# A kernel of block attention and a feed-forward network whose planner is given other durations and preferences

## The chip, the core and the metric

The kernel runs on one core of a Trainium2 chip. The core has five engines that run side by side, each through its own list of instructions in order: TensorE (PE) multiplies matrices and transposes, ScalarE (ACT) applies functions and copies, VectorE (DVE) does elementwise work, reductions and 32 x 32 transposes, GpSimd (POOL) does elementwise work and issues some transfers, and SyncE (SP) issues most transfers (DMA). Engines wait for each other by semaphores. The metric is the time of one execution on the device in microseconds (us), lower being better.

## The reference

The inputs q, k and v are 8 x 8 x 576 x 64 float32 numbers (batch, heads, sequence, head size), the weights 512 x 2048 and 2048 x 512. The weights come as float64 arrays, which the kernel receives as 8-byte words and turns into float32 itself.

```python
scores = scale * np.matmul(q_c, k_c.transpose(0, 1, 2, 4, 3))   # blocks of 64 positions
scores = scores - np.max(scores, axis=-1, keepdims=True)
attn = np.exp(scores)
attn = attn / (np.sum(attn, axis=-1, keepdims=True) + 1e-09)
out = np.matmul(attn, v_c)
...
x = np.ascontiguousarray(attn_out.transpose(0, 2, 1, 3)).reshape(B * S, H * D)
...
h = x @ w_in
g = h * (1.0 / (1.0 + np.exp(-1.702 * h)))
return (g @ w_out).astype(np.float32)
```

Each block of 64 positions attends to itself alone. The 4608 rows of the result, 512 wide, go through a feed-forward network of width 2048.

## The kernel before

**Tiles.** The 4608 rows are 36 tiles of 128 rows, in nine blocks of four tiles. The width 2048 is 16 slices j of 128. For a block n and a slice j, numbered g = 16 n + j, the kernel makes h (128 x 512), its activation g, and adds four products, one per tile of the block, to four output accumulators. A float32 product is made of three: each operand is split into a high part and a low rest (`g_h` and `g_l`, `x_h` and `x_l`, two halves of `w`), and high x high, high x low and low x high are summed. Blocks 0 to 2 are computed plainly. The other six go in twos, where seven products (`P1` to `P7`, line 698 on) take the place of eight.

**Names of steps.** Each step has a name by which the text speaks of it. For the first four attention tiles u: `q_u`, `k_u`, `v_u` are loads (256 KB each, line 368), `tqp_u` and `tkp_u` transposes on PE (line 407), `tq_u` and `tk_u` the copies of these (lines 412, 416 on ACT, 418 on DVE), `s_u` the scores (line 428), `m_u`, `sm_u` maximum and subtraction on DVE, `ex_u` the exponential on ACT (441), `z_u` the sum (445 to 448), `n_u` the division on POOL (451), `ep_u` the transposes of the weights of attention on PE (456), `et_u` their copy (463), `xp_u` the product with v (472), and `xh_u`, `xl_u` its two parts (480, 483). From tile 4 on, tiles go in pairs with like names; their rows come by `rows0_4` and `rows1_4` and are transposed by `tp0_4` and `tp1_4` (891) in pair 4, and in later pairs they come in small loads `qk_i_n_u` (866) that DVE transposes (`tq0_u`, `tq1_u`, 909). From pair 8 on `s_u` also holds the product with v of the pair before. For the weights of slice j: `raw_j` is two loads (288 and 292, 512 KB each), `wsc_j` and `wlow_j` two steps on ACT (296, 300), `wshift_j` and `wj_j` two on DVE (305, 309), `wh_j` one on ACT (314) and `w_j` the last on DVE (319). For the feed-forward: `h0_g` and `h_g` are halves of the first product (1160 to 1162; for the first two slices 1171 to 1173, by halves of the columns, `h_0_0` the very first), `gh_g` the activation and its high part (1181, 1182), `gl_g` the rest (1187), and `o_g_t` the product for tile t (1197 to 1199). `fill_0` to `fill_2` and `warm` are matmuls without use, which keep PE busy (1272); `gt` loads the table of the activation (1276).

**What sets the order.** All steps are handed to a planner, class `Plan`, with engine, an assumed duration, a rank, the steps that they need and the buffers that they take and give. `emit` (line 99) plays the plan through: whenever an engine is free it takes, of the steps whose needs are met and whose buffers are free, the one with the lowest rank. A step's end is told to other engines `HANDOVER` later. The resulting sequence is the program order of every engine; the hardware takes no part in it and an engine that meets a step whose input isn't there waits, with everything behind it. Two tables bend the order: `NUDGE` adds to the rank of single steps, `SHIFT` to those of a whole pair. For the first 20 to 50 steps of each engine the table `ORDER` (line 22) writes the order out.

```python
rank += self.nudge.get(make, 0.0) + self.shift
...
turn = name == first[e][-1] if first.get(e) else name not in listed
if turn and all(self.free[b] >= take.count(b) for b in take):
    pick = i
...
plan.add(DMA, (2, 1.5, 384), rank - 5.5, load, need=need, make=e("raw"), take=[f"w{j}"])
plan.add(ACT, 1.08, rank, scale, need=[e("raw")], make=e("wsc"))
```

## Time and profile before

| what | value |
|---|---|
| median of 3 runs | 825.58 us (823.32 to 827.49) |
| profiled execution | 828.46 us, its span 826.7 us |
| instructions in the span | 14873 |
| granted TensorE clock | 1.000 |
| DMA moved | 114.24 MB, mean 138 GB/s |

The span goes from the first to the last instruction; 1.8 us of the profiled execution lie around it. A row of the timeline has start, length, engine, line of the program, operation, what is written from what, shape and number of instructions, and in brackets idle time of the engine before it and what ended it. PE's lengths are modelled, and neighbours overlap, so the text counts from start to start.

### The profile page before, as it was taken

The page shows a single profiled execution, that of the slowest core. Times are in us where ns is not written, and L with a number is a line of the kernel's source. Part 1 is how long each engine was busy: PE and PEld are TensorE (multiplying, and loading weights), DVE is VectorE, ACT ScalarE, POOL GpSimd, SP SyncE. Part 2 cuts the span into 40 slices and gives each one's busy share as a digit, 9 for nine tenths or more (in the row PEclk, how much of TensorE's full clock was granted, in tenths as well). Part 3 has the DMA queues.
Part 4 walks back from the last instruction along what each step waited for, and adds up shares of the span by engine and source line. Part 5 has one row for each costly group of instructions (what it writes and reads, how often), then busy time and mean ns, then how long its engine had stood idle before and what let it go on. Part 6 is the DMA issues. An engine that isn't in the chain of part 4 may idle for free.

```text
span 826.7 us, 14873 instructions
## 1 busy us (share of the span) xinstructions
PE 814.1 (98%) x5750; PEld 673.2 (81%) x5750; DVE 525.8 (64%) x725; ACT 370.9 (45%) x545; POOL 137.7 (17%) x170
## 2 busy tenths in 40 slices
PE   8899999999999999999999999999999999999998
PEld 7778787888888888888888888888888888888886
DVE  5868975664487768873958874857568443443422
ACT  5989745323445537433436434434454323222322
POOL 1000172112176422030203030200010010000100
PEclk9999999999999999999999999999999999999999
DMA  8997855532385356756655255655440054444101
GB/s 214 334 278 218 291 156 126 90 60 39 71 270 155 82 169 198 180 144 171 165 155 144 51 102 166 155 142 144 122 141 26 1 178 127 117 117 123 52 1 51
DMA packets 219237, 114.24 MB, mean 138 GB/s; under 512 B 172640, under 2 KB 195424, under 8 KB 219168
## 3 DMA queue, kind: packets, MB, share of 16 engines
q1 hardware_dynamic: 214624, 103.20, 47.4%
q0 software_dynamic: 4544, 10.10, 3.7%
q8 instruction: 45, 0.74, 0.4%
q14 instruction: 24, 0.20, 0.1%
HBM read 89.13 MB, written 24.12 MB: 137 GB/s over the span
## 4 chain that ended last, share of the span: by engine, by line
PE 82%; SPq 9%; DMA 4%; ACT 2%; DVE 2%; issue 1%; POOL 0%; DVEq 0%
PE po L1197 14%; PE po L1199 14%; PE po L1198 14%; PE hp L710 9%; PE hp L712 9%; PE hp L711 9%; PE hp L1160 3%; PE hp L1161 3%; PE hp L1162 3%; DMA raw<-in_moe_w_out_dram 3%; SPq L368 2%; SPq L288 2%; SPq L866 2%; PE s L925 2%; PE x L999 2%; SPq L292 1%
## 5 line engine op out<-in xcount | busy, mean ns | idle before, releaser
L1197 PE MATMUL po<-w,g_l 128*128 128x512 f32 x576 | 226.4, 393 | 0.3 <-DVE g_l L1187 0.2
L1199 PE MATMUL po<-w,g_h 128*128 128x512 f32 x576 | 224.3, 389 | 0.0
L1198 PE MATMUL po<-w,g_h 128*128 128x512 f32 x576 | 224.3, 389 | 0.0
L1197 PEld LDWEIGHTS po<-w,g_l 128*128 128x128 f32 x576 | 108.1, 188 | 23.8 <-DVE g_l L757 0.5
L1199 PEld LDWEIGHTS po<-w,g_h 128*128 128x128 f32 x576 | 108.1, 188 | 22.7
L1198 PEld LDWEIGHTS po<-w,g_h 128*128 128x128 f32 x576 | 108.1, 188 | 21.8
L710 PE MATMUL hp<-w,w 128*128 128x512 f32 x224 | 87.2, 389 | 0.0
L712 PE MATMUL hp<-w,w 128*128 128x512 f32 x224 | 87.1, 389 | 0.0
L711 PE MATMUL hp<-w,w 128*128 128x512 f32 x224 | 87.1, 389 | 0.0
L974 DVE STREAM_TRANSPOSE eT<-e 32x512 f32<-32x512 f32 x120 | 84.2, 702 | 4.6 <-POOL e L955 2.7
L748 ACT ACTIVATE g<-g 128x512 f32<-128x512 f32 x48 | 30.1, 632 | 124.8 <-DVE g L695 124.4
L1160 PE MATMUL hp<-x_l,w 128*128 128x512 f32 x184 | 72.1, 392 | 1.6 <-DVE g_l L1187 1.5
L1161 PE MATMUL hp<-x_h,w 128*128 128x512 f32 x184 | 71.6, 389 | 0.0
L1162 PE MATMUL hp<-x_h,w 128*128 128x512 f32 x184 | 71.6, 389 | 0.0
L1216 POOL DMA_DIRECT2D out_dram<-ob x35 | 19.4, 557 | 294.7 <-DVE ob L1211 222.8
L753 ACT ACTIVATE g_h<-g 128x512 fp32r<-128x512 f32 x48 | 30.3, 630 | 72.5 <-PE po L1199 71.4
L757 DVE TENSOR_TENSOR g_l<-g,g_h 128x512 fp32r<-128x512 f32 x48 | 33.1, 690 | 44.4 <-ACT g_h L753 44.1
L1187 DVE TENSOR_TENSOR g_l<-hp,g_h 128x512 fp32r<-128x512 f32 (+1 forms) x50 | 33.2, 665 | 37.9 <-ACT g_h L1182 37.6
L909 DVE STREAM_TRANSPOSE qkT<-raw 128x1024 f32<-128x1024 f32 x30 | 36.9, 1237 | 27.7 <-PE s L925 18.1
L866 POOL DMA_DIRECT2D raw<-in_k_dram x44 | 26.3, 600 | 151.7 <-DMA v<-in_v_dram 80.3
L710 PEld LDWEIGHTS hp<-w,w 128*128 128x128 f32 x224 | 42.0, 188 | 8.9 <-ACT d L723 0.2
L712 PEld LDWEIGHTS hp<-w,w 128*128 128x128 f32 x224 | 42.0, 188 | 8.7
(120 smaller groups left out, 1254.3 us busy)
## 6 DMA issues: line engine op xcount, KB each, us to landing
w<-seven SPq DMA_DIRECT2D x112, 256.0 KB, 2.8
pieces<-seven SPq DMA_DIRECT2D x56, 256.0 KB, 2.8
seven<-w SPq DMA_DIRECT2D x24, 512.0 KB, 4.0
raw<-in_moe_w_in_dram SPq DMA_DIRECT2D x16, 512.0 KB, 7.4
raw<-in_moe_w_out_dram SPq DMA_DIRECT2D x16, 512.0 KB, 7.7
out_dram<-ob POOLq DMA_DIRECT2D x27, 256.0 KB, 2.6
raw<-in_q_dram SPq DMA_DIRECT2D x208, 32.0 KB, 2.2
v<-in_v_dram SPq DMA_DIRECT2D x26, 256.0 KB, 3.4
```

The source lines that it names most:

```text
L710: nc.tensor.matmul(hp, w[:, 0, c], xl[:, c], start=c == 0, stop=False)
L711: nc.tensor.matmul(hp, w[:, 0, c], xh[:, c], start=False, stop=False)
L712: nc.tensor.matmul(hp, w[:, 1, c], xh[:, c], start=False, stop=c == 1)
L866: queue.dma_start(t[p0 : p0 + 32, i, n, o // 32 : (o + c) // 32, :], src[b, 2 * n + h, s : s + c, d * 32 : d * 32 + 32].rearrange("(t j) i ...
L909: nc.vector.transpose(st["tr"][:, i].rearrange("p n (t j) -> p (n t) j", j=32), st["raw"][:, i].rearrange("p n t j -> p (n t) j"),)
L974: nc.vector.transpose(st["et"][po : po + 32, :, 32 * a : 32 * a + 32], st["e"][pi : pi + 32, :, 32 * b : 32 * b + 32],)
L1160: nc.tensor.matmul(hp, wh, xl, start=cc == 0, stop=False)
L1161: nc.tensor.matmul(hp, wh, xh, start=False, stop=False)
L1162: nc.tensor.matmul(hp, wl, xh, start=False, stop=cc == NCC - 1)
L1197: nc.tensor.matmul(po, gl[:, c], w[:, 0, :], start=first, stop=False)
L1198: nc.tensor.matmul(po, gh[:, c], w[:, 0, :], start=False, stop=False)
L1199: nc.tensor.matmul(po, gh[:, c], w[:, 1, :], start=False, stop=last)
```

## The change

The durations that the planner assumes are changed for some twenty kinds of steps (by -0.3 to +0.6 us); and a step on ACT or DVE now holds its engine 0.08 less, while its result counts for other engines 0.20 after that (0.12 before) and for its own engine 0.08 after it. `NUDGE` gets some twenty new entries, `SHIFT` has twelve instead of six, and `ORDER` is written anew. No instruction is added, removed or altered.

```diff
@@ ORDER, ACT @@
-        "tk_1 tq_1 tq_0 ex_1 tq_2 tk_2 ex_0 tq_3 tk_3 ex_2 et_1 wsc_0 wlow_0 xh_1 ex_3 et_0 et_2 "
+        "tq_1 tk_1 tq_0 tk_2 ex_1 tq_2 tq_3 ex_0 wsc_0 wlow_0 tk_3 ex_2 et_1 xh_1 ex_3 wsc_1 et_0 "
...
@@ ORDER, DMA @@
-        "k_1 q_1 k_0 q_0 q_2 k_2 q_3 k_3 raw_0 v_1 v_0 v_2 raw_1 v_3 raw_3 raw_2 rows0_4 raw_4 "
+        "q_1 q_0 k_1 k_0 k_2 q_3 q_2 raw_0 k_3 v_1 raw_1 v_3 v_2 v_0 rows0_4 raw_3 raw_2 raw_4 "
...
-    HANDOVER = {None: 0.0, PE: 0.25, ACT: 0.12, DVE: 0.12, POOL: 0.15, DMA: 0.1}
+    HANDOVER = {None: 0.0, PE: 0.25, ACT: 0.2, DVE: 0.2, POOL: 0.15, DMA: 0.1}
+    OVERLAP = {ACT: 0.08, DVE: 0.08}
...
+        if engine in self.OVERLAP:
+            cost -= self.OVERLAP[engine]
...
-                        post(done + late, 1, (make, e, True))
+                        post(done + late + self.OVERLAP.get(e, 0.0), 1, (make, e, True))
...
+        "o_123_3": 8.5, "P3_2_7": 8, "wsc_12": -1, "qk_1_2_10": 2, "d3_0_0": 1, "h0_18": 1, "t4x_2_0": -2,
     }
-    SHIFT = {10: 3.5, 8: 2.0, 26: -12.5, 12: 4.0, 34: -12.5, 6: 3.0}
+    SHIFT = {10: 1.5, 8: 2.0, 26: -12.5, 12: 4.0, 34: -3.0, 6: 2.0, 32: 9.0, 18: -9.0, 30: 12.5, 22: 2.0, 28: 16.5, 20: 1.0}
...
-        plan.add(DMA, (2, 1.5, 384), rank - 5.5, load, need=need, make=e("raw"), take=[f"w{j}"])
+        plan.add(DMA, (2, 1.6, 384), rank - 5.5, load, need=need, make=e("raw"), take=[f"w{j}"])
```

Three places show what the new order does. Six lines were put in near the top of the program, so a line L296 of before is L302 in the changed kernel, and so on. In the rows the first number in a tile's name is the tile or slice.

SP's list of transfers at the beginning, from the eighth one on; before:

```order
L368 DMA first_a_3_121<-in_k_dram 128x8x64
L288 DMA raw_0_157<-in_moe_w_in_dram 128x4x128
L292 DMA raw_0_157<-in_moe_w_out_dram 128x512
L368 DMA first_b_1_150<-in_v_dram 128x8x64
L368 DMA first_b_0_188<-in_v_dram 128x8x64
L368 DMA first_b_2_225<-in_v_dram 128x8x64
L288 DMA raw_1_274<-in_moe_w_in_dram 128x4x128
L292 DMA raw_1_274<-in_moe_w_out_dram 128x512
L368 DMA first_b_3_298<-in_v_dram 128x8x64
```

and now:

```order
L294 DMA raw_0_129<-in_moe_w_in_dram 128x4x128
L298 DMA raw_0_129<-in_moe_w_out_dram 128x512
L374 DMA first_a_3_113<-in_k_dram 128x8x64
L374 DMA first_b_1_170<-in_v_dram 128x8x64
L294 DMA raw_1_178<-in_moe_w_in_dram 128x4x128
L298 DMA raw_1_178<-in_moe_w_out_dram 128x512
L374 DMA first_b_3_223<-in_v_dram 128x8x64
L374 DMA first_b_2_236<-in_v_dram 128x8x64
L374 DMA first_b_0_189<-in_v_dram 128x8x64
```

The first weights go ahead of k_3, the second ahead of three of the v loads, and v_0 from second to last of these.

ACT's list at the same place, from ex_0 on (line 441 before, 447 now; tile 0); before:

```order
L441 ACTIVATE first_b_0_188<-first_b_0_188 128x512
L412 ACTIVATE first_a_3_121<-qkTp_3_0_190 128x512
L416 ACTIVATE first_a_3_121<-qkTp_3_1_220 128x512
L441 ACTIVATE first_b_2_225<-first_b_2_225 128x512
L463 ACTIVATE first_b_1_150<-eTp_1_232 128x512
L296 ACTIVATE raw_0_157<-raw_0_157 128x1024
L300 ACTIVATE raw_0_157<-raw_0_157 128x1024
L480 ACTIVATE x_h_0_83<-x_1_281 128x4x128
L441 ACTIVATE first_b_3_298<-first_b_3_298 128x512
L463 ACTIVATE first_b_0_188<-eTp_0_301 128x512
```

and now:

```order
L447 ACTIVATE first_b_0_189<-first_b_0_189 128x512
L302 ACTIVATE raw_0_129<-raw_0_129 128x1024
L306 ACTIVATE raw_0_129<-raw_0_129 128x1024
L422 ACTIVATE first_a_3_113<-qkTp_3_1_231 128x512
L447 ACTIVATE first_b_2_236<-first_b_2_236 128x512
L469 ACTIVATE first_b_1_170<-eTp_1_251 128x512
L486 ACTIVATE x_h_0_83<-x_1_288 128x4x128
L447 ACTIVATE first_b_3_223<-first_b_3_223 128x512
L302 ACTIVATE raw_1_178<-raw_1_178 128x1024
L469 ACTIVATE first_b_0_189<-eTp_0_280 128x512
```

wsc_0 and wlow_0, the two steps on raw_0, stand ahead of tk_3, ex_2 and et_1 now, and wsc_1 ahead of et_0.

PE's list around tp1_4, the transposes of pair 4's second rows; before:

```order
L1197 MATMUL po_0_3_533<-w_3_543,g_l_3_630 128x512
L1198 MATMUL po_0_3_533<-w_3_543,g_h_3_629 128x512
L1199 MATMUL po_0_3_533<-w_3_543,g_h_3_629 128x512
L891 MATMUL qkTp_4_1_671<-ident_73,rows_4_330 128x128 x8
L1160 MATMUL hp_5_686<-x_l_0_84,w_5_644 128x512
```

and now:

```order
L897 MATMUL qkTp_4_1_661<-ident_73,rows_4_306 128x128 x8
L1203 MATMUL po_0_3_498<-w_3_563,g_l_3_617 128x512
L1204 MATMUL po_0_3_498<-w_3_563,g_h_3_616 128x512
L1205 MATMUL po_0_3_498<-w_3_563,g_h_3_616 128x512
L1166 MATMUL hp_4_620<-x_l_0_84,w_4_583 128x512
```

o_3_3 and the second half of h of slice 4 (h_4, six matmuls, of which the last row is the first) come behind the transposes now; before, both came ahead of them.

More of the change, by code (lines that the diff above doesn't have):

```diff
@@ L487, in plan_first @@
         rank = u - 95
[L488 to L492 removed]
+        plan.add(DMA, (1, 1.05, 1024), u - 103, lambda: load(0), make=ev("q"), take=[slot(0)])
+        plan.add(DMA, (1, 1.05, 1024), u - 102.9, lambda: load(1), make=ev("k"))
+        plan.add(DMA, (1, 1.05, 1024), u - 101.5, load_v, make=ev("v"), take=[slot(1)])
+        plan.add(PE, 0.62, rank, lambda: t_pe(0), need=[ev("q")], make=ev("tqp"), take=["hp"])
+        plan.add(PE, 0.62, rank, lambda: t_pe(1), need=[ev("k")], make=ev("tkp"), take=["hp"])
         plan.add(ACT, 0.55, rank, t_q, need=[ev("tqp")], make=ev("tq"), give=["hp"])
         plan.add(ACT if k_act else DVE, 0.62, rank, t_k, need=[ev("tkp")], make=ev("tk"), give=["hp"])
[L495 removed]
+        plan.add(PE, 1.08, rank + 0.6, s_pe, need=[ev("tq"), ev("tk")], make=ev("s"), take=[f"po{u}"], give=[slot(0)])
         plan.add(DVE, 0.71, rank + 0.6, s_max, need=[ev("s")], make=ev("m"))
@@ L639, in plan_prep @@
             plan.bulk((1.5, 0.85)[i], first - PREP, lambda i=i: out_a(i), need=[(w0, w1)[i]], make=outs[i])
-        plan.add(POOL, 1.05, rank, lambda: whole(0), need=[w0, f"w_{NF - 1}"], make=e("pa0"), take=["tmp"])
-        plan.add(POOL, 1.05, rank, lambda: whole(1), need=[w1, e("pa0")], make=e("pa"))
-        plan.add(POOL, 2.4, rank, sums, need=[e("pa")], make=e("psum"), take=["tmp"], give=["tmp"])
+        plan.add(POOL, 1.27, rank, lambda: whole(0), need=[w0, f"w_{NF - 1}"], make=e("pa0"), take=["tmp"])
+        plan.add(POOL, 1.27, rank, lambda: whole(1), need=[w1, e("pa0")], make=e("pa"))
+        plan.add(POOL, 3.0, rank, sums, need=[e("pa")], make=e("psum"), take=["tmp"], give=["tmp"])
         for i in range(2):
@@ L761, in plan_two @@
             at = rank + STEP * i / 7
-            plan.bulk(0.72, at - LEAD, lambda k=k, i=i: load(k, i), need=[f"po_{p}"], make=e(f"ld{i}"), take=[f"piece{k}"])
+            plan.bulk(0.8, at - LEAD, lambda k=k, i=i: load(k, i), need=[f"po_{p}"], make=e(f"ld{i}"), take=[f"piece{k}"])
             xneed = [f"l{OPERANDS[name][1]}x_{s}_{h}" for h in range(2)] if p == 0 else []
@@ L765, in plan_two @@
             plan.add(
-                PE, 1.36, at - 0.2, lambda k=k, i=i: product(k, i), need=[e(f"ld{i}"), before] + xneed, make=e(name),
+                PE, 1.362, at - 0.2, lambda k=k, i=i: product(k, i), need=[e(f"ld{i}"), before] + xneed, make=e(name),
                 take=["hp"], give=[f"piece{k}"],
@@ L1092, in plan_pair @@
             plan.add(
-                PE, 2.2, rank + 0.6, lambda: (s_pe(), last["x"][0]()), need=both + [ev("hp0"), ev("hp1")],
+                PE, 2.04, rank + 0.6, lambda: (s_pe(), last["x"][0]()), need=both + [ev("hp0"), ev("hp1")],
                 make=ev("s"), take=["att", "att", "e"], give=["tr", "et", "v"],
@@ L1101, in plan_pair @@
         plan.add(DVE, 1.65, rank + 0.6, s_sum, need=[ev("ex")], make=ev("z"))
-        plan.add(POOL, 2.0, rank + 0.6, s_norm, need=[ev("z")], make=ev("n"))
+        plan.add(POOL, 1.9, rank + 0.6, s_norm, need=[ev("z")], make=ev("n"))
         if pe:
-            plan.add(PE, 0.95, rank + 1.7, e_pe, need=[ev("n")], make=ev("ep"), take=["att", "att"], give=["e"])
+            plan.add(PE, 0.82, rank + 1.7, e_pe, need=[ev("n")], make=ev("ep"), take=["att", "att"], give=["e"])
             plan.add(ACT, 1.05, rank + 1.7, e_act, need=[ev("ep")], make=ev("et"), take=["et"], give=["att", "att"])
@@ L1114, in plan_pair @@
             plan.add(
-                PE, 1.4, rank + 1.5, x_pe, need=part["x"][1], make=ev("xp"), take=bank, give=["et", "v"],
+                PE, 1.1, rank + 1.5, x_pe, need=part["x"][1], make=ev("xp"), take=bank, give=["et", "v"],
             )
@@ L1242, in plan_ffn @@
         else:
-            plan.add(PE, 1.37, g - 0.2, lambda: h_pe(0), need=need, make=ev("h0"), take=["hp"])
-            plan.add(PE, 1.37, g - 0.2, lambda: h_pe(1), need=[ev("h0")], make=ev("h"), give=last)
+            plan.add(PE, 1.362, g - 0.2, lambda: h_pe(0), need=need, make=ev("h0"), take=["hp"])
+            plan.add(PE, 1.362, g - 0.2, lambda: h_pe(1), need=[ev("h0")], make=ev("h"), give=last)
             plan.add(ACT, 1.18, g - 5, g_hi, need=[ev("h")], make=ev("gh"), take=["g"], table="gelu")
@@ L1276, in gelu_table @@
         nc.scalar.activation(z[:, :1], ident[:, :1], AF.Gelu_apprx_sigmoid)
-    plan.add(PE, 3.4, -1000, lambda: keep_warm(ps_o, "po3", WARM), make="warm")
+    plan.add(PE, 3.75, -1000, lambda: keep_warm(ps_o, "po3", WARM), make="warm")
     for i, n in enumerate(FILL):
         plan.add(
-            PE, 0.23 * n, -1000, lambda n=n: keep_warm(ps_h, "hp", n), make=f"fill_{i}", take=["hp"], give=["hp"],
+            PE, 0.276 * n, -1000, lambda n=n: keep_warm(ps_h, "hp", n), make=f"fill_{i}", take=["hp"], give=["hp"],
         )
```

24 lines of the change are left out of this document (9 added, 15 removed), and 18 rows, old and new, of tables (NUDGE, ORDER).

## Prediction

> **What bounds the kernel now.** I read the page first, then the busy time by stretches, then the instructions of TensorE (PE) in order of time at every gap, and last what ScalarE (ACT) and the DMA queue did before those gaps.
>
> ```profile
> PE 814.1 (98%) x5750; PEld 673.2 (81%) x5750; DVE 525.8 (64%) x725; ACT 370.9 (45%) x545; POOL 137.7 (17%) x170
> 0.00:24.00 24.00, 19.39 (x298) 17.11 (x302) 13.97 (x26) 14.37 (x21) 4.88 (x10) 1.00 0.88 231
> 24.00:55.00 31.00, 28.45 (x204) 24.01 (x194) 21.62 (x27) 26.70 (x38) 0.00 (x0) 1.00 0.96 289
> 55.00:146.00 91.00, 89.37 (x690) 72.85 (x691) 71.14 (x84) 61.03 (x75) 28.02 (x29) 1.00 0.72 210
> 146.00:823.00 677.00, 676.85 (x4576) 559.23 (x4574) 419.08 (x591) 268.25 (x412) 104.77 (x131) 1.00 0.45 118
> ```
>
> Columns are the stretch, its length, busy time of PE, weight loads, VectorE (DVE), ACT and GpSimd (POOL) with their counts, the granted clock, the DMA share and GB/s. The reader should see that from 146 us to 823 us PE has nothing left to give (676.85 of 677), and no instruction is added or removed. So an order can win only what PE lost before 146 us, and can lose wherever a new wait opens. The DMA share stands at 0.88 to 0.96 until 55 us: the beginning is bound by transfers and by ACT, which waits for them in its written order.
>
> Gaps are read from start to start. A 512-column matmul holds PE for 0.23 us, four transposes in a row for 0.42 and the 64 small matmuls of a pair's scores for 1.09 (58.38 to 59.47).
>
> ```profile
> 52.53 0.39 PE L1198 MATMUL po<-w,g_h 128*128 128x512 f32 x1
> 52.76 0.39 PE L1199 MATMUL po<-w,g_h 128*128 128x512 f32 x1
> 54.22 0.63 PE L891 MATMUL qkTp<-ident,rows 128*128 128x128 f32 x4 [1.08 <-DMA rows<-in_q_dram]
> 55.03 0.66 PE L891 MATMUL qkTp<-ident,rows 128*128 128x128 f32 x4 [0.18 <-DMA rows<-in_k_dram]
> 55.45 0.48 PE L1160 MATMUL hp<-x_l,w 128*128 128x512 f32 x1
> ...
> 58.38 1.16 PE L925 MATMUL s<-qkT 64*64 64x64 f32 x64
> 59.47 0.50 PE L1197 MATMUL po<-w,g_l 128*128 128x512 f32 x1
> ...
> 83.35 0.39 PE L1199 MATMUL po<-w,g_h 128*128 128x512 f32 x1
> 83.85 0.50 PE L1160 MATMUL hp<-x_l,w 128*128 128x512 f32 x1
> ...
> 94.95 1.16 PE L925 MATMUL s<-qkT 64*64 64x64 f32 x64
> 97.01 0.50 PE L1160 MATMUL hp<-x_l,w 128*128 128x512 f32 x1 [0.90 <-DVE g_l L1187]
> ...
> 142.82 0.39 PE L1199 MATMUL po<-w,g_h 128*128 128x512 f32 x1
> 143.79 0.50 PE L1160 MATMUL hp<-x_l,w 128*128 128x512 f32 x1 [0.59 <-DVE g_l L1187]
> ...
> 327.22 0.39 PE L1199 MATMUL po<-w,g_h 128*128 128x512 f32 x1
> 327.65 0.50 PE L710 MATMUL hp<-w,pieces 128*128 128x512 f32 x1
> ...
> 778.66 0.39 PE L1199 MATMUL po<-w,g_h 128*128 128x512 f32 x1
> 779.14 0.50 PE L1197 MATMUL po<-w,g_l 128*128 128x512 f32 x1
> ```
>
> The waits behind the start are 1.23 (54.22 - 52.76 - 0.23) and 0.39 (55.03 - 54.22 - 0.42) for the rows of pair 4, then 0.27, 0.97, 0.74, 0.20 and 0.25: together 4.05 us. This is the purse for which the new order plays. The other account is the start, up to the first matmul of the feed-forward at 24.67 us.
>
> **The start, step by step.** The rows that carry it:
>
> ```profile
> 15.14 0.59 ACT L463 ACTIVATE first_b<-eTp 128x512 f32<-128x512 f32 x1
> 17.24 1.15 ACT L296 ACTIVATE raw<-raw 128x1024 f32<-128x1024 f32 x1 [1.51 <-DMA raw<-in_moe_w_out_dram]
> 18.28 1.17 ACT L300 ACTIVATE raw<-raw 128x1024 int32<-128x1024 uint32 x1
> ...
> 21.30 1.07 ACT L314 ACTIVATE w<-wtmp 128x1024 fp32r<-128x1024 f32 x1
> 22.24 0.61 ACT L480 ACTIVATE x_h<-x 128x512 fp32r<-128x512 f32 x1
> 22.87 1.28 ACT L1276 ACT_TABLE_LOAD   x1
> ...
> 23.49 1.21 DVE L319 TENSOR_TENSOR w<-wtmp,w 128x1024 fp32r<-128x1024 f32 x1
> ...
> 18.06 0.69 PE L472 MATMUL x<-first_b 64*64 64x64 f32 x32 [0.57 <-DMA first_b<-in_v_dram]
> ...
> 24.67 0.36 PE L1171 MATMUL hp<-x_l,w 128*128 128x256 f32 x1
> ...
> 0.00:14.00 14.00, 11.80 (x142) 10.41 (x142) 5.20 (x10) 6.17 (x10) 1.36 (x7) 1.00 0.92 230
> 14.00:18.00 4.00, 3.05 (x46) 2.62 (x46) 3.75 (x9) 2.22 (x4) 2.15 (x3) 1.00 0.53 124
> ```
>
> ACT runs its list in the written order. Now wsc_0 (L296) waits for raw_0, the first weights, after tk_3, ex_2 and et_1 are done. In the new list wsc_0 and wlow_0 stand ahead of those three, so tiles 1, 2 and 3 of the first attention hang on raw_0 as well.
>
> When does raw_0 land? By 14 us the DMA has moved 14 x 230 = 3.22 MB, while eight loads of 0.262 MB and raw_0 with 1.05 MB make 3.15. The bytes have passed, yet ACT is let go only at 17.24, and between 14 and 18 us the DMA is half idle (0.53): a tail of 3.3 us. In the new queue one small load (k_3) goes behind raw_0: 0.262 MB at 230 GB/s, 1.1 us. With the whole tail raw_0 lands at 16.1, without any at 12.6; I take 14.5, the middle. wsc_0 and wlow_0 (1.15 and 1.17, 0.1 of it overlapped) then end at 16.7, tk_3 and ex_2, as long as et_1's 0.59, at 17.9, and et_1, with a short wait for PE, near 18.8 (15.73 now). xp_1 used to wait for v_1 until 18.06, so about 1.5 us are lost there.
>
> The second arm is v_0, which goes from second of the four v loads to last, behind raw_1. Ahead of its end lie twelve small loads and two weights, 5.24 MB; the first 24 us move 5.54 MB, so they have passed at 22.7, and with a tail between 0 and 3.3 they land between 22.7 and 26.0; I take 23.8. From there xp_0 (0.69 on PE), xh_0 (0.61) end at 25.2 with two handovers of 0.05; the first arm arrives at about the same time, through wsc_1 and the 1.28 of the table load, which both now stand ahead of xh_0. Behind xh_0 stand wh_0 (1.07) and w_0 on DVE (1.21), which used to be ahead of it or beside it: 27.6 with a handover of 0.1. The first feed-forward matmul goes from 24.67 to 27.6: **2.9 us later**. The new list also has wsc_4 ahead of gh_1_0 and wh_2, one more L296 (1.04 from start to start, 18.28 - 17.24), of which 0.1 may fall into a gap, so w_2 and with it h0_2 are later by another 0.9. Sum of the start: **+3.8**, bounds +1.8 (no tail: 1.1 less for v_0, and the 0.9 not paid) and +6.0 (the whole tail: 26.0 for v_0).
>
> PE may stand still for long in this stage: the new list puts tkp_3, the transpose of k_3, ahead of ep_1 and of the fill matmuls, and k_3 comes behind raw_0, at about 15.5, while s_2 is through at about 13 (13.11 now). That is a gap of 2.5 us, up to 4 with the whole tail; the waits there now are of 1.4 us at most.
>
> ```profile
> 1.37 3.35 PE L1272 MATMUL warm<-ident 128*128 128x128 f32 x14 [1.37 <-POOL ident masks.py:199]
> 4.51 2.57 PE L407 MATMUL qkTp<-ident,first_a 128*128 128x128 f32 x12
> ...
> 11.96 1.15 PE L428 MATMUL s<-first_a 64*64 64x64 f32 x32 [0.25 <-ACT first_a L416]
> ...
> 16.10 1.38 PE L1272 MATMUL warm<-ident 128*128 128x128 f32 x10
> ```
>
> After its first idle stretch PE needs 5.7 us for 26 matmuls (1.37 to 7.08), at the later pace of 0.14 each they would take 3.6. So a relapse costs at most 2.1 us, and nothing where PE waits anyway; I take 0. [...]
>
> **Pair 4 and the later waits.** Each transfer ahead of pair 4's second rows is the same in both queues, so they land as now: 54.22 for q, 55.03 for k. But o_3_3 (0.68, three matmuls) and h_4 (1.36, six) go from before their transposes to behind. PE is ready for these at 52.99 - 2.04 + 3.8 = 54.75, so q costs nothing more, and k is there when the first four transposes end. The late start has eaten both waits (1.62), and it covers the others that hang on transfers and on ACT: with them today's waits come to 1.62 + 0.27 + 0.97 + 0.74 = 3.60, less than 3.8. They have also shorter chains: raw_13 goes ahead of qk_1_0_6, and v0_8 goes behind three groups of pair 10's loads that follow it today. The two small waits behind 146 us (0.45) keep their neighbours in the new order; I keep them.
>
> **The products.** s_22 goes ahead of four products and two output steps, 4 x 1.36 + 2 x 0.68 = 6.8 us of PE, and pair 20 has to end by then.
>
> ```profile
> 306.00:342.00 36.00, 35.96 (x221) 29.41 (x213) 32.22 (x47) 19.95 (x31) 6.54 (x9) 1.00 0.68 186
> 338.96 1.43 DVE L974 STREAM_TRANSPOSE eT<-e 32x512 f32<-32x512 f32 x2
> 342.16 1.16 PE L925 MATMUL s<-qkT 64*64 64x64 f32 x64
> ```
>
> It would start at 335.4. Its last input ends now at 340.4; four DVE steps ahead of it go behind (3.4 us), and DVE has 36 - 32.2 = 3.8 us idle there, of which m_20's earlier place can give any part: 333.2 to 337.0. The wait is 0 to 1.6; I take 0, since ex_20 and z_20 go up by six places too. s_12 and s_28 go later, by five and eight microseconds of PE steps, which gives their own inputs more time. All other moves are within lists whose readers wait nowhere today (0.15 us idle in 677), and cost nothing while that holds; if the cover were gone, one DVE step of 0.7 us each time.
>
> **Sum.** 826.7 + 3.8 + 0.45 - 4.05 + 0 = 826.9 us of span, 0.2 more than now. The profiled execution took 828.5 with 1.8 outside the span, and the median of the runs is 825.58, so what it lost at the start is on the large side. The difference carried over gives 825.8.
>
> **Rivals.**
>
> *The start is no later.* If raw_0 and v_0 land without any tail, and s_0 and ep_0, which go ahead in the new PE list, pay as well, the start costs 0 to 1.8, pair 4's rows land early too, and all 4.05 are saved: 825.58 - 4.05 + 0 to 1.8 = 821.5 to 823.3. For it speaks the half idle DMA from 14 to 18 us; against it that wsc_0 then still binds three tiles to raw_0. Chance 0.25; a little over half of it beyond 0.5%.
>
> *ACT stands at wsc_0.* The tail stays whole, and each microsecond of raw_0 behind 14.5 passes through tk_3, s_3, xp_1 and xh_0 into h_0_0. At raw_0 = 14.3 the change breaks even; at 17.24, as today, the start is 3.8 + 2.7 = 6.5 late and the time is 825.58 + 6.5 + 0.45 - 4.05 = 828.5. For it: today's 17.24. Against: k_3 less in front. Chance 0.18; beyond 0.5% (raw_0 after 18.5) in under half of it.
>
> *PE's pace falls back.* The gap ahead of tkp_3 lets the slow pace of the first 5.7 us return while ep, xp and h_0_0 run: up to 2.1 us, 827.9. For it the length of the gap, against it that PE waits for most of the next 10 us. Chance 0.05, all within 0.5%. [...]
>
> *The pairs are too near.* s_22 waits 1.6, and since P5_0_1 behind it waits for DVE too, 3 us in all: 828.8. For it DVE's 32.2 of 36 us; against it the 3.8 idle. Chance 0.08; beyond 0.5% in a third of it.
>
> The rest, 0.44, is the forecast: the start pays the purse back.
>
> **Numbers.** 0.5% is 4.1 us, about what a measurement here can tell from no change. Faster by more: 0.15 (from the first rival and a little of the forecast). Slower by more: 0.13. Within: 0.72. The range reaches from the first rival's 821.5, less 0.5 for the spread of the runs, to the second's 828.5 with the 1.6 of s_22 on top: 821.0 to 830.1. The likeliest case's own range is 824 to 827.5.
>
> **What would show it.** In the new profile: wsc_0 (first instruction of its line on ACT) at 14 to 16 us with a wait for the DMA, and tk_3 behind it; a gap on PE of 2 us or more ahead of tkp_3; the first matmul with 256 columns at 26 to 29.5 us; no wait for pair 4's rows, or under 0.5 us; no gap near 84, 97 and 144 us; PE busy again 676 of 677 us from 146 on; s_22 at about 335 us without a wait. I am wrong if h_0_0 starts at 25 us or earlier (then it is faster), if raw_0 lands after 17 us, or if gaps open behind 146 us. If short matmuls at 18 to 24 us go at the pitch of the first ones, the pace has fallen back.

## The result and the profile after

The changed kernel takes **834.91 us** (median of 6 runs, 833.48 to 837.34), the kernel before beside it 825.51 (823.32 to 827.61). The ratio is 1.0113, with a 95% interval from 1.0089 to 1.0136: **slower by 9.4 us**. 825.8 was forecast, with a range up to 830.1. The profiled execution took 835.50 us.

The busy times of the whole execution, and by the same stretches as before (length, PE, weight loads, DVE, ACT, POOL, granted clock, DMA share, GB/s):

```profile
PE 818.2 (98%) x5750; PEld 675.9 (81%) x5750; DVE 526.8 (63%) x725; ACT 370.9 (44%) x545; POOL 138.9 (17%) x170
0.00:24.00 24.00, 18.52 (x274) 16.55 (x274) 12.33 (x24) 13.46 (x20) 5.60 (x10) 0.99 0.95 239
24.00:55.00 31.00, 29.14 (x219) 24.92 (x211) 23.13 (x28) 28.06 (x37) 0.07 (x1) 0.90 1.01 325
55.00:146.00 91.00, 91.00 (x700) 74.74 (x699) 72.98 (x86) 60.34 (x76) 28.77 (x29) 1.00 0.68 196
146.00:830.00 684.00, 679.45 (x4573) 559.65 (x4571) 418.37 (x589) 268.47 (x412) 104.50 (x131) 1.00 0.44 117
```

The third stretch went as forecast: PE is busy 91.00 of 91.00 us, every wait of before is gone. The last one did not. It is 684 us long instead of 677, and 4.6 us of it are idle (0.15 before). The rows of PE behind these gaps, in order of time (start, length, what; idle time and what ended it):

```profile
325.94 0.51 PE L1203 MATMUL po<-w,g_l 128*128 128x512 f32 x1 [3.07 <-ACT ob L1215]
336.35 0.50 PE L716 MATMUL hp<-w,w 128*128 128x512 f32 x1 [0.29 <-DVE d L701]
463.28 0.50 PE L1203 MATMUL po<-w,g_l 128*128 128x512 f32 x1 [0.45 <-DVE g_l L763]
503.91 0.50 PE L716 MATMUL hp<-w,w 128*128 128x512 f32 x1 [0.65 <-DVE g L701]
```

From start to start, less the pitch of 0.23, these are 3.23, 0.45, 0.61 and 0.81 us. The first is `o_48_2`. Together they are 5.1 us, and the half clock behind the first (327.25 to 330.66, below) adds 1.6. The chain of waits leads from `o_48_2` through ACT to an output store:

```profile
318.15 0.70 DVE ob L1217
318.86 0.41 issue
319.26 5.88 DMA out_dram<-ob
...
325.30 0.60 ACT ob L1215
325.90 0.04 issue
325.94 0.51 PE po L1203
```

The step `ob_2_2` on ACT copies an accumulator out, so that `o_48_2` may fill it again. It needs one of two output buffers, and that is free once the store `st_2_1` has landed, 5.88 us after its issue.

At the start the forecast rows are there:

```profile
13.79 1.14 ACT L302 ACTIVATE raw<-raw 128x1024 f32<-128x1024 f32 x1
...
15.84 0.61 ACT L422 ACTIVATE first_a<-qkTp 128x512 f32<-128x512 f32 x1
...
23.25 1.00 PE L478 MATMUL x<-first_b 64*64 64x64 f32 x32 [2.07 <-ACT gelu L1282]
...
24.30 0.60 ACT L486 ACTIVATE x_h<-x 128x512 fp32r<-128x512 f32 x1 [1.04 <-PE x L478]
...
27.44 0.58 PE L1177 MATMUL hp<-x_l,w 128*128 128x256 f32 x1
```

wsc_0 starts at 13.79, tk_3 behind it, and the first feed-forward matmul at 27.44 us (24.67 before). It takes 0.58 instead of 0.36, and the granted clock is 0.50 there, from 23.46 to 30.29 us. The row at 23.25 is xp_0. It names ACT's table step as what ended the wait, but et_0 had ended at 21.74; what came last by the trace is v_0, issued at about 16.4 and landed 6.7 us later.

### The profile page after: what moved, and what is told of

Same layout as the page of the kernel before. It is cut to its first block, busy times and chain, and to the rows that moved or that the text cites. A ratio compares the mean times of both kernels' runs of the same rounds, so it can differ in the third digit from the quotient of the medians.

```text
span 833.7 us, 14836 instructions
## 1 busy us (share of the span) xinstructions
PE 818.2 (98%) x5750; PEld 675.9 (81%) x5750; DVE 526.8 (63%) x725; ACT 370.9 (44%) x545; POOL 138.9 (17%) x170
## 4 chain that ended last, share of the span: by engine, by line
PE 92%; DVE 4%; DMA 1%; ACT 1%; SPq 1%; issue 0%; DVEq 0%; ACTq 0%
PE po L1203 15%; PE po L1204 15%; PE po L1205 15%; PE hp L716 9%; PE hp L718 9%; PE hp L717 9%; PE hp L1166 5%; PE hp L1167 5%; PE hp L1168 5%; PE s L931 2%; PE x L1005 2%; DVE eT L980 2%; DMA first_a<-in_k_dram 1%; DMA out_dram<-ob 1%; SPq L374 1%; DVE g_l L763 1%
## 5 line engine op out<-in xcount | busy, mean ns | idle before, releaser
L961 POOL TENSOR_TENSOR e<-e,r 128x1024 f32<-128x1024 f32 x16 | 32.3, 2018 | 121.1 <-DVE r L958 70.8
L716 PEld LDWEIGHTS hp<-w,w 128*128 128x128 f32 x224 | 42.2, 188 | 11.0 <-DVE d L701 1.2
L1187 ACT ACTIVATE hp<-hp 128x512 f32<-128x512 f32 (+1 forms) x50 | 28.5, 569 | 49.1 <-PE hp L1168 40.3
```

The lines of the kernel that those rows point to most:

```text
L716: nc.tensor.matmul(hp, w[:, 0, c], xl[:, c], start=c == 0, stop=False)
```

## The experiments

What the planner makes is a sequence of named steps. In all kernels below but before_again this sequence is given as a list, in which single steps are moved and all others stay; durations and preferences play no part there. Written out unmoved, the lists give the two kernels' own orders.

Each kernel was timed beside the kernel before, whose median lay between 824.17 and 825.51 us in the different rounds, so kernels are compared by the ratio, not by their medians. Two numbers stand for each profile: when `h_0_0` starts, and how long PE needs from the first matmul of `s_10` (scores of pair 10, about 150 us) to its last matmul. The second number splits the kernel into start and rest.

| kernel | median, ratio to before (interval) | h_0_0 | s_10 | s_10 to the end |
|---|---|---|---|---|
| before, first profile | 825.51 | 24.67 | 152.18 | 670.42 |
| before_again | 823.71 (one run) | 24.35 | 147.80 | 670.04 |
| the changed kernel | 834.91, 1.0113 (1.0089 to 1.0136) | 27.44 | 151.52 | 678.16 |
| late_of_before | 828.44, 1.0044 (1.0029 to 1.0059) | 30.40 | 156.32 | 670.60 |
| late_of_after | 831.58, 1.0073 (1.0053 to 1.0093) | 23.93 | 148.96 | 676.56 |
| start_of_before | 825.97, 1.0009 (0.9994 to 1.0023) | 24.19 | 147.64 | 670.32 |
| late_stores_in_old | 827.21, 1.0037 (1.0024 to 1.0049) | 24.16 | 148.44 | 672.39 |
| new_from_400 | 827.23, 1.0031 (1.0017 to 1.0044) | 23.93 | 148.29 | 672.50 |
| weight_stores_earlier | 835.21, 1.0136 (1.0109 to 1.0163) | 27.02 | 150.39 | 677.04 |
| weight_stores_both | 834.95, 1.0128 (1.0106 to 1.0150) | 31.15 | 154.62 | 676.16 |
| weight_stores_third | 833.49, 1.0109 (1.0082 to 1.0136) | 25.91 | 150.22 | 675.56 |
| output_later | 835.60, 1.0117 (1.0099 to 1.0135) | 31.26 | 154.76 | 676.57 |
| three_steps | 835.76, 1.0117 (1.0090 to 1.0144) | 26.60 | 150.38 | 675.18 |
| both_mended | 833.57, 1.0103 (1.0088 to 1.0119) | 26.27 | 151.00 | 675.89 |
| stores_and_outputs | 835.98, 1.0137 (1.0120 to 1.0154) | 26.66 | 151.14 | 676.87 |
| wait_filled | 837.42, 1.0149 (1.0126 to 1.0171) | 30.76 | 156.69 | 678.84 |
| start_v0_earlier | 829.81, 1.0054 (1.0035 to 1.0073) | 28.48 | 152.99 | 670.02 |
| start_filled | 827.00, 1.0036 (1.0024 to 1.0048) | 27.34 | 150.58 | 670.04 |
| start_k3_first | 827.92, 1.0041 (1.0026 to 1.0055) | 27.16 | 151.39 | 670.09 |
| start_scale_later | 828.46, 1.0048 (1.0030 to 1.0066) | 30.33 | 153.88 | 670.09 |

### Where the time goes: the order cut in two

```diff
 late_of_before:  steps up to s_10 as in the changed kernel, the rest as before
 late_of_after:   steps up to s_10 as before, the rest as in the changed kernel
 start_of_before: steps up to h_3 as before, then as changed up to s_10, the rest as before
```

> The new order up to the scores of pair 10 (153.5 us in its trace), and from there on the rest of the steps in the old order, engine by engine. Theory A: the new order loses behind 320 us, where single DVE steps stand behind the work of pairs 20, 26 and 28 and pass their lateness to PE; up to 154 us it is level or up to 0.7 us ahead. Then this kernel takes 824 to 826.5 us, PE has no wait over 0.3 us behind 154 us, and the granted clock is half only at 23 to 30 us. Rival B: the later start and the half clock at 23 us are what costs, and the late gaps only sit where PE would wait anyway: 832 to 835 us.

> The mirror image: the old order up to the scores of pair 10, the new one from there on. Theory A: the gaps at 322, 336, 462 and 503 us come back at the same steps, half clock after the first: 825.5 + 7.7 = 832 to 834 us. Rival B: no late start, so no loss: 824.5 to 826.5 us.

> The old order for the start (all steps up to h_3 on PE), then the new one up to the scores of pair 10, then the old one again. If the start was forecast rightly, h_0_0 is at 24.7 us again and the clock is not halved; of the 3.6 us of waits between 54 and 144 us, those for pair 4's rows come back (1.6), the other 2.0 stay away in part: 822.5 to 825, I take 823.7. If the waits are all gone by the new order itself, 821.5; if they all come back because they were only covered by the late start, 825.5.

The new start alone costs 1.0044 (3.6 us of 825), the new rest alone 1.0073 (6.0 us); together 9.6, the measured 9.4. So both theories had half of it: theory A named gaps that do cost time, but its claim that the start is level fell; rival B was right that the start costs, and wrong that it is all. With all starts, the old order takes 670.0 to 670.6 us from s_10 on, and the new one 675.2 to 678.8. The new order between h_3 and s_10 neither wins nor loses anything that can be measured (1.0009).

### Was there a purse?

```diff
 before_again: the kernel before, unchanged
```

> The kernel before, unchanged, for a second profile. The first one (828.46 us) was 2.9 above the median of the runs. Theory A1: its waits of 3.6 us between 52 and 144 us belonged to that execution and not to the order; a second profile near 825 us has under 1.5 us of them, so the purse of the prediction was mostly not there, which is why the later start isn't paid back. Rival: the waits are of the order and stand there again with 3 to 4 us.

It took 823.71 us. Its two stretches from 55 us on:

```profile
55.00:146.00 91.00, 91.00 (x700) 75.02 (x699) 72.37 (x86) 60.51 (x75) 28.03 (x29) 1.00 0.70 195
146.00:818.00 672.00, 671.91 (x4557) 555.75 (x4555) 416.51 (x587) 266.97 (x410) 104.64 (x131) 1.00 0.45 118
```

PE is busy 91.00 of 91.00 us, in the old order. The five waits between 52 and 144 us that the prediction added up to 3.6 us belonged to the first profiled execution. Three more profiles with the old order in that stretch say the same: late_of_after has none of these waits, late_stores_in_old one of 0.51 at 140 us, new_from_400 one of 0.72 there. That is also why start_of_before gains nothing (825.97, and 823.7 was expected): its new middle had no waits to take away. before_again lay 1.8 us below the median beside it (825.47), so a run in the middle may still lose some of it; no profile shows how much. With nothing to win back, the forecast would have been 825.6 + 3.8 = 829.4 us.

### The place at 320 us

The two 512 KB stores of weights, `pouts0_7` and `pouts1_7` (line 631, now 637), are issued later in the new order. SP's transfers, before and after:

```profile
313.89 0.34 SPq L631 DMA_DIRECT2D seven<-w  x1
315.40 0.37 SPq L701 DMA_DIRECT2D pieces<-seven  x1
315.87 1.68 SPq L631 DMA_DIRECT2D seven<-w  x1
```

```profile
314.75 0.37 SPq L707 DMA_DIRECT2D pieces<-seven  x1
316.78 0.36 SPq L707 DMA_DIRECT2D w<-seven  x1
317.25 1.20 SPq L637 DMA_DIRECT2D seven<-w  x2
```

They hang on `plo0_7` and `plo1_7` on DVE, which now stand behind m_20, l5x_0_1 and ob_2_3, and on SP they stand behind two loads, of which the second waits for its buffer until 316.78. The two issues of the last row are at 317.25 and 318.1, so the stores are 3.4 and 2.2 us later. The reverse experiment makes only these two late, in the old order:

```diff
-DVE, before:        gl_47 plo0_7 l4x_0_1 plo1_7 d1_0_0 ob_2_3 l5x_0_1 ob_2_1
+late_stores_in_old: gl_47 l4x_0_1 d1_0_0 ob_2_3 plo0_7 l5x_0_1 plo1_7 ob_2_1
-SP, before:         ld6_0_0 pouts0_7 ld0_0_1 pouts1_7 ld1_0_1
+late_stores_in_old: ld6_0_0 ld0_0_1 pouts0_7 pouts1_7 ld1_0_1
```

> The old order whole with only these two stores made late: on SP pouts0_7 behind ld0_0_1, on DVE plo0_7 behind ob_2_3 and plo1_7 behind l5x_0_1, so that they are issued some 3.4 and 2.2 us later, as in the new order. Theory A2: h6x stands on ACT ahead of ob_2_0, so PE waits 2.5 to 3.5 us at o_48_0 or P4_0_0: 825.3 + 3 = 828.3, between 827 and 830. Rival (the stores are only one of many): 825 to 826.5.

3.0 us slower, as expected (1.0037). The stores went at 313.71 and 314.9, in before_again at 309.50 and 311.48. Rows of the kernel before, and then ACT of late_stores_in_old:

```profile
319.11 0.63 ACT L562 ACTIVATE w<-xs 128x512 fp32r<-128x512 f32 x1 [1.68 <-DMA seven<-w]
...
321.72 1.21 ACT L1209 ACTIVATE ob<-po 128x512 f32<-128x512 f32 x2 [1.46 <-DMA out_dram<-ob]
...
323.37 0.39 PE L1197 MATMUL po<-w,g_l 128*128 128x512 f32 x1
```

```profile
317.00 0.63 ACT L568 ACTIVATE w<-xs 128x512 fp32r<-128x512 f32 x1 [3.23 <-DMA seven<-w]
...
320.59 0.60 ACT L1215 ACTIVATE ob<-po 128x512 f32<-128x512 f32 x1 [1.96 <-DVE w L571]
```

h6x_0_0 writes where the stores read and waits 3.23 us for them (1.68 before). PE's largest wait, 0.92 us at 321, comes another way, though. It hangs on ob_2_2, the row at 320.59, and that starts when the output store st_2_1 lands, issued at 315.87 and 4.6 us under way; the row names a DVE step, as the rows of ob_2_2 in output_later and both_mended do, but there, too, ob_2_2 starts within 0.2 us of that landing. This store takes 3.6 and 3.2 us in the two profiles of the kernel before and 5.9 in the changed kernel. So late weight stores alone are enough to lengthen the output store and to cost 3 us, by another wait than the expected one at h6x_0_0. Where they cost it is seen only in part: PE of this profile waits 0.30, 0.92 and 0.45 us at 316, 321 and 326 us, 1.7 together, and its last stretch is 2.4 longer than in before_again. Taking them away in the new order was harder. Three tries:

```diff
-DVE, changed kernel:    t4x_0_1 l5x_0_1 l2x_0_1 d1_0_0 ob_2_3 plo0_7 d2_0_0 plo1_7 ob_2_1
+weight_stores_earlier:  t4x_0_1 plo0_7 d1_0_0 plo1_7 ob_2_3 l5x_0_1 l2x_0_1 d2_0_0 ob_2_1
+weight_stores_both:     t4x_0_1 plo0_7 l2x_0_1 plo1_7 d1_0_0 ob_2_3 l5x_0_1 d2_0_0 ob_2_1
+weight_stores_third:    t4x_0_1 l5x_0_1 plo0_7 plo1_7 d1_0_0 ob_2_3 l2x_0_1 d2_0_0 ob_2_1
-SP, changed kernel:     ld6_0_0 ld0_0_1 ld1_0_1 pouts0_7 pouts1_7
+_both and _third:       ld6_0_0 pouts0_7 ld0_0_1 pouts1_7 ld1_0_1
```

> The new order whole but for one place on DVE at 313 us: plo0_7 and plo1_7, on which the two 512 KB stores of weights (seven<-w) hang, go ahead of the steps l5x_0_1, l2x_0_1, as in the old order. Theory A, its first link: the late stores of weights crowd the output store st_2_1 (5.9 us instead of under 3.8), which holds the output buffer, ACT's ob_2_2 and PE's o_48_2. Then the gap of 3.2 us at 322 us goes and with it the half clock at 327 to 331 us: 834.9 - 4.8 = 830.1, between 829.5 and 831.5. Rival: ob_2_2 is late because of its own place on ACT, ahead of h6x_0_0, and the store takes as long as it does: the gap stays, 834 to 836 us.

> The new order whole, with the two stores of weights pouts0_7 and pouts1_7 (seven<-w) put early on both engines that hold them: on SP ahead of the loads ld0_0_1 and ld1_0_1, as in the old order (weight_stores_earlier left that out, and they were issued at 318.4 and 318.9 us all the same), and on DVE plo0_7 and plo1_7 right behind t4x_0_1. Theory A2: these stores are the root at 322 us, by their traffic beside the output store and because h6x writes where they read. Issued at 314.5 and 316 they leave a gap of at most 1 us and no half clock: 834.9 - 2.5 - 1.5 = 831, between 830 and 832. Rival: the stretch is too full on DVE whatever its order (the three mends so far only moved the gap), and 2 us or more of waits appear within 20 us: 833.5 to 836.

> As weight_stores_both, but with l5x_0_1 left where the new order has it; in both earlier kernels it went behind ob_2_3, and P6_0_0, which multiplies with it, waited 2.1 us. Now l2x_0_1, which P5_0_0 needs 3 us later, goes behind instead. Theory A2: neither the gap at P6_0_0 nor that at o_48_2 is there, the half clock at 327 us neither; the three DVE gaps behind 330 us stay: 834.9 - 4 = 830.9, between 829.8 and 832. Rival: another wait of over 1.5 us appears within 20 us: 833 to 836.

The first edit did not reach its aim: on SP the stores still stood behind the load, and were issued at 318.4 and 318.9 us. In the second they went at 317.3 and 318.6, ahead of a PE that was itself 3 us later, and the gap at o_48_2 and the half clock were gone. But in both l5x_0_1 had gone behind ob_2_3, and P6_0_0, which needs it, waited 2.1 us; this was a fault of the edit, put right in the third. There the last stretch is 2.6 us shorter than in the changed kernel's profile (678.16 - 675.56), but the ratio is 1.0109 against 1.0113, 0.3 us and well within the intervals (4 us were expected). What is left stands on ACT:

```profile
320.69 0.60 ACT L1215 ACTIVATE ob<-po 128x512 f32<-128x512 f32 x1 [2.83 <-DMA out_dram<-ob]
322.94 0.60 ACT L1215 ACTIVATE ob<-po 128x512 f32<-128x512 f32 x1 [1.65 <-DMA out_dram<-ob]
```

The output store st_2_1 still took 4.8 us. Why it did, with the weight stores out of the way, is not shown. And PE comes to o_48_2 sooner: the new order has P6_0_0 ahead of o_47_0 to o_47_2 where it was behind them. From the end of o_47_1, whose result that store writes, to o_48_2 there are now a o_47, two products and two o_48 (3 x 0.68 + 2 x 1.36 = 4.8 us) instead of 6.1. The chain over copy, store and ob_2_2 needs 7.8 us in the changed kernel's profile (318.13 to 325.94), and 5.2 with the 3.3 us that the same store took at most in before_again (issued 314.17, ob_2_2 from 317.5). So even with a store of that length some 0.4 us of wait would be left in the new order (an estimate). The other half of the place, then, the output steps behind more of PE's work, alone and with the first:

```diff
-PE, changed kernel:   P5_0_0 o_48_0 o_48_3 o_48_2 P3_0_0 o_48_1 P4_0_0
+output_later:         P5_0_0 P3_0_0 o_48_0 o_48_3 P4_0_0 o_48_2 o_48_1
+stores_and_outputs:   P5_0_0 P3_0_0 o_48_3 o_48_0 P4_0_0 o_48_2 o_48_1
-ACT, changed kernel:  ob_2_0 ob_2_2 h6x_0_0 h6x_0_1
+both:                 ob_2_0 h6x_0_0 h6x_0_1 ob_2_2
-DVE, changed kernel:  d3_0_0 tq1_22 d4_0_0 l6x_0_0 l6x_0_1
+output_later:         d3_0_0 l6x_0_0 l6x_0_1 d4_0_0 tq1_22
+stores_and_outputs:   d3_0_0 d4_0_0 l6x_0_0 l6x_0_1 tq1_22, and weight_stores_third
```

> The new order whole but for one place at 320 us: on PE the products P3_0_0 and P4_0_0 go ahead of the output steps o_48_0 to o_48_2, as in the old order, on ACT ob_2_2 goes behind h6x, and on DVE l6x and d4_0_0 ahead of tq1_22. The store st_2_1 may take as long as it does, PE reaches the accumulator 3 us later. Theory A: the gap at 322 us (3.2) and the half clock behind it (1.6) go: 834.9 - 4.8 = 830.1, between 829 and 831.5. Rival: ACT still stands at ob_2_2, and ge_65 and what follows hold PE a little later: 833 to 835.

> The new order whole with the two halves of the place at 320 us undone together: the weight stores early on SP and DVE (as weight_stores_third), and the output steps back behind products (PE: P3_0_0 o_48_3 o_48_0 P4_0_0 o_48_2 o_48_1 behind P5_0_0; ACT: h6x between ob_2_0 and ob_2_2; DVE: d4_0_0 and l6x ahead of tq1_22). Each half alone left 2 us of waits (2.1 and 2.7 between 318 and 330 us). Theory A3: the new order put both sides closer, the output steps on PE 1 to 2 us nearer and the stores 2 to 3 us later, and only both together take the gap away: at most 1 us of waits between 318 and 330 us, no half clock at 327 us, 834.9 - 4 = 830.9, between 829.8 and 832. Rival: the stretch is too full in any order that keeps the new places of pair 20 (ex_20 on ACT at 314 us with two table loads of 1.28, z_20 and tq1_22 on DVE): 833 to 835.

("As in the old order", in the first of these, is true of P4_0_0 alone; what differs in the old order is the place of P6_0_0, and putting that back alone wasn't tried.) Neither is faster than the changed kernel. In output_later P4_0_0 waits 2.4 us for the drain d4_0_0, which stands behind l6x on DVE, and l6x waits for h6x, which on ACT stands for the late weight stores:

```profile
326.40 0.63 ACT L568 ACTIVATE w<-xs 128x512 fp32r<-128x512 f32 x1 [2.80 <-DMA seven<-w]
```

In stores_and_outputs these are early, o_48_2 doesn't wait, but l6x_0_0 itself takes four times as long as usual (DVE, POOL, then PE):

```profile
323.27 2.79 DVE L571 TENSOR_TENSOR w<-xs,w 128x512 fp32r<-128x512 f32 x1 [0.82 <-ACT w L568]
323.59 1.92 POOL L961 TENSOR_TENSOR e<-e,r 128x1024 f32<-128x1024 f32 x1
...
326.72 0.50 PE L716 MATMUL hp<-w,pieces 128*128 128x512 f32 x1 [2.43 <-DVE w L571]
```

The step of 0.69 us meets n_20 on POOL and ends 0.55 us after that has ended. Each mend took one wait away, and the next in line showed up within 10 us, as large. What the place needs as a whole is open, and so is which step of the new order is the root here; the old order as a whole has no wait.

### The places behind 330 us

```diff
-DVE, changed kernel: et1_20 et2_20 d1_0_1 ... et_26 t1x_1_0 gl_67 ... et2_28 et_28 d4_1_0
+three_steps:         et1_20 d1_0_1 et2_20 ... et_26 gl_67 t1x_1_0 ... et2_28 d4_1_0 et_28
 both_mended: output_later and three_steps together
 new_from_400: steps up to P1_0_6 (400 us) as before, the rest as in the changed kernel
```

> The new order whole but for three places on DVE: d1_0_1 ahead of et2_20, gl_67 ahead of t1x_1_0, d4_1_0 ahead of et_28. Theory A: the gaps at 336 (0.45), 462 (0.61) and 503 us (0.81) go, the one at 322 stays: 834.9 - 1.9 = 833.0, between 832.3 and 834. Rival: what goes behind is waited for in its turn (et_20, et_28 are needed by the scores of the next pair): 834 to 836.

> Both edits together. Theory A: nothing is left of the loss behind 154 us, and only the start remains: as with the old order from 153 us on, 828.4, between 827.3 and 829.5. Rival: the gaps move elsewhere: 831 to 834.

> The old order up to P1_0_6 on PE (400 us), the new one from there on, so that only the places at 462 and 503 us and the small ones behind them are of the new order. By the gaps in its trace these are worth 0.61 + 0.81 + 0.3 = 1.7 us: 824.8 + 1.7 = 826.5, between 825.8 and 827.3. Rival: the loss behind 154 us is spread over all of the new order, half of the 6.4 us lying behind 400: 828.

three_steps doesn't get faster (1.0117): of the gaps at 462 and 503 us 0.26 and 0.59 stay, and the one at 336 moves on to o_49_0. both_mended is 0.8 us below the changed kernel by the ratio (1.0103 against 1.0113, within the intervals), not 6.5, and still has gaps of 1.64, 0.47, 0.60 and 0.83 us. new_from_400 costs 1.0031, 2.5 us, within its interval the expected 1.7. So of the 6.0 us behind s_10 some 2.5 lie behind 400 us and, by subtraction, 3.5 between s_10 and 400, where the new profile has no gaps but those at 326 and 336.

Why gl_67 is late at 462 us can be read, though no run tries it. From 447.78 to 463.14 us DVE has no idle time, and one step is long:

```profile
449.40 0.63 DVE L763 TENSOR_TENSOR g_l<-g,g_h 128x512 fp32r<-128x512 f32 x1
449.63 2.15 POOL L961 TENSOR_TENSOR e<-e,r 128x1024 f32<-128x1024 f32 x1 [0.79 <-DVE r L958]
449.94 2.39 DVE L571 TENSOR_TENSOR w<-xt,w 128x512 fp32r<-128x512 f32 x1
...
462.54 0.69 DVE L763 TENSOR_TENSOR g_l<-g,g_h 128x512 fp32r<-128x512 f32 x1
```

A step of 0.69 us took 2.39 beside n_26 on POOL. Without these 1.7 us DVE would have come to gl_67 1.1 us ahead of need instead of 0.6 behind (an estimate). In new_from_400 the same step takes 2.39, too; in before_again a step of this line and form takes 0.68 there (440.69).

### Is the half clock caused by the wait?

```diff
-PE, changed kernel: o_48_0 o_48_3 o_48_2
+wait_filled:        o_48_0 o_48_3 (26 matmul calls without use) o_48_2
```

> The new order whole with 26 matmuls of 128 columns without use ahead of o_48_2, in its gap of 3.2 us at 322 us. If the half clock at 327 us comes from PE standing still, it is gone, the wait itself stays: 834.9 - 1.5 = 833.4, between 832.5 and 834.2. If it comes from something else, it stays there: 834 to 836.

The edit was twice too large: a call is two matmuls (PE counts 5802 against 5750), 52 of 0.107 us, 5.6 us in a gap of 3.2. The excess of 2.4 us is about what the kernel is slower by (1.0149 against 1.0113, 3.0 us). PE had no gap there, and the clock stayed whole at 327 us; but it stays whole in other kernels with that gap as well (below), so this run doesn't decide the question, and the price of the half clock remains the one of the trace: eight matmuls at 0.43 instead of 0.23, 1.6 us, in two of the ten profiles with the new order there.

### What makes the start late

All four have the order of late_of_before (1.0044), with one thing changed, in start_v0_earlier two:

```diff
-SP, new start:          q_2 raw_0 k_3 v_1 raw_1 v_3 v_2 v_0
+start_v0_earlier:       q_2 raw_0 k_3 v_1 v_0 raw_1 v_3 v_2
+start_k3_first:         q_2 k_3 raw_0 v_1 raw_1 v_3 v_2 v_0
-ACT, new start:         ex_0 wsc_0 wlow_0 tk_3 ex_2 et_1 xh_1 ex_3 wsc_1 et_0 gt xh_0 wh_0
+start_v0_earlier:       ex_0 wsc_0 wlow_0 tk_3 ex_2 et_1 xh_1 ex_3 wsc_1 et_0 xh_0 wh_0 gt
+start_scale_later:      ex_0 tk_3 ex_2 et_1 wsc_0 wlow_0 xh_1 ex_3 wsc_1 et_0 gt xh_0 wh_0
-PE, new start:          tkp_3 ... xp_0 ep_3 xp_2 h_0_0
+start_filled:           (6 calls) tkp_3 ... (7 calls) xp_0 ep_3 (5 calls) xp_2 h_0_0
```

> The kernel of late_of_before (new start, old order from 153 us on) with two places of the start undone: v_0 goes second of the v loads, ahead of raw_1, and on ACT xh_0 and wh_0 go ahead of the table load gt. Theory A: h_0_0 hangs on v_0, as the prediction had it; xp_0 at 21 us instead of 22 to 26, h_0_0 at 25 to 26 instead of 26.6 to 31.3, and the time is 828.4 - 2.5 = 825.9, between 825 and 827. Rival: ACT is held by wsc_0 anyway and the start stays 3 us late: 828 to 829.5.

> The kernel of late_of_before with matmuls without use (6, 7 and 5 calls, each two matmuls of 128 columns) put into PE's list ahead of tkp_3, xp_0 and xp_2, where it stands still. Theory S1: the start loses by the half clock that follows these gaps; in the profiles with a gap of 2.3 to 3.0 us ahead of tkp_3 the clock is halved at 15 us for 6.8 us and h_0_0 is at 30.4 to 31.3, without it at 26.3 to 28.5. With the gaps filled the clock stays whole, h_0_0 is at 26 to 27.5 and the time 826.5, between 825.7 and 827.5. Rival: the transfers set the start, and the time stays at 828 to 830.

> The kernel of late_of_before with k_3 again ahead of raw_0 in SP's queue. Theory S2: the start loses because k_3 lands behind raw_0; tkp_3 then waits 0.6 to 3.0 us, and tk_3, s_3 and the third tile behind it. Put back, the gap ahead of tkp_3 is under 0.6 us, no half clock at 15 us, wsc_0 is some 1 us later, h_0_0 at 26 to 27.5: 826.5, between 825.7 and 827.5. Rival: what tkp_3 gains wsc_0 loses on ACT: 828 to 830.

> The kernel of late_of_before with wsc_0 and wlow_0 again behind tk_3, ex_2 and et_1 on ACT, SP's queue as new. Theory S3: ACT's two steps of 2.1 us ahead of tk_3 make tiles 1 to 3 late: xh_1 comes 1 to 2 us earlier with this edit, h_0_0 too, and the time is 827, between 826 and 828. Rival S2: tk_3 waits for k_3 now, and wsc_0 behind it: no gain, 828 to 830.

v_0 is not the last to come: with v_0 early h_0_0 still was at 28.48, right behind xp_2, which stands ahead of it on PE and waited for et_2. The chain in that profile comes from raw_1, which v_0 had put back: it lands at 21.32, and behind it ACT goes through wsc_1, wh_0 and the table load to et_2 at 26.87. k_3 and ACT's order, each put back alone, gain nothing either (1.0041, 1.0048). Filling the gaps gains 0.7 us at the most likely: the clock stayed whole to PE's end (1.000 over the profile), and the ratio is 1.0036, but the intervals of both overlap, so this gain is not shown; 3.0 us of the 3.6 remain. So none of these four edits takes the loss of the start away, and its cause stays open beyond the new order of the start as a whole.

What the profiles show is two kinds of starts. Of ten with the new order unmodified there, four had the clock halved from about 15 us for 6.8 us, behind 2.1 to 2.9 us of idle PE ahead of tkp_3 (0.2 to 1.2 in the others), which waits for k_3; in these h_0_0 starts at 30.4 to 31.3, in the six others at 25.9 to 27.4 (mean 26.7). With the old start it is 23.9 to 24.7 in six profiles (mean 24.2). The 4.2 us between the two kinds (30.9 and 26.7) can be split: tkp_3 itself starts at 16.5 on average in the four and at 14.8 in the six, because k_3 lands later, and from there to h_0_0 it takes 14.4 and 11.9 us. So 1.7 us are there before the clock falls, and 2.5 come behind it.

## Why the prediction was wrong, point by point

**The purse failed.** "The waits behind the start are ... together 4.05 us. This is the purse for which the new order plays." It was read correctly, but from one execution, which lay 2.9 us above the median of the runs; in the four other profiles with the old order there the same waits come to 0 to 0.7. The prediction saw the 2.9 ("what it lost at the start is on the large side") and carried it over as a constant; it should have taken it off the purse. This term was mis-sized by some 3 us, and with it the sum by as much.

**The start was right in size, in part by luck.** h_0_0 was forecast at 27.6 and came at 27.44, while ten profiles of this start lie between 25.9 and 31.3; PE as a whole "+3.8" late, and at s_10 the changed kernel's profile is 3.7 behind before_again (151.52 - 147.80), and by the ratio the new start costs 3.6. Its arms were only half right: that xh_0 follows v_0 held (xp_0 at 23.25, forecast near 24), but start_v0_earlier shows that another chain, over raw_1, ACT's list and et_2, ends as late. wsc_0 at 13.79 and raw_0's landing were within the forecast's 12.6 to 16.1.

**The pace was mis-sized, but not by much.** "So a relapse costs at most 2.1 us, and nothing where PE waits anyway; I take 0", with a chance of 0.05. In all ten profiles of the new start the clock was halved at some point between 23 and 30 us, and in four at 15 us too; in those four h_0_0 came 4.2 us later than in the rest, of which 2.5 lie behind the relapse. So the price was near its bound and the chance far too low. The clock can fall with the old start as well: in late_of_after it was halved from 28.15 to 31.57 us. In the median it counts for little: filled gaps gain 0.7 at the most likely.

**Pair 4 and the later waits**: none in the new profile, as forecast; but none in before_again either.

**The products.** s_22 was to start at 335.4 without a wait; it started at 339.99 without one, 4.6 us later because of the gaps and the half clock ahead of it. That step held, and the rival "the pairs are too near" was at the right place with the wrong wait: it looked at s_22 and P5_0_1, while PE came to wait for the accumulator of o_48_2 and for the drain d1_0_1.

**"All other moves ... cost nothing while that holds" failed**, by 6.0 us; 0.7 for each lost cover was the largest price named. The reason given was that their "readers wait nowhere today (0.15 us idle in 677)". An idle time of nothing says that nobody is late, not how near each is. At 320 us the new order moved two things at once: o_48_2 nearer to o_47_1 by one product, 6.1 to 4.8 us, and the weight stores back by 3.4 and 2.2 us. The rows of before would have shown how near the wait was: ob_2_2, the second of the two copies at 321.72, ends at 322.93 and o_48_2 starts at 323.37, 0.4 us later. One product less (1.36) or an output store longer by 1 us already opens a wait. The prediction followed s_22 at this place, and neither P6_0_0 nor SP's list past the start. The prediction's sign "if gaps open behind 146 us" is what came.

**The sum**, remade with what the runs showed: start 3.6 and rest 6.0 are 9.6 us, measured 9.4. In the forecast's own terms, the +3.8 of the start stands, the moves put at 0 cost 6.0, and of the 4.05 next to nothing came back.
